# The order of the last five adds and stores of a fused attention and gMLP kernel

## The chip, the core and the metric

The kernel runs on one core of a Trainium2 chip. The metric is the device time of one execution in microseconds, the median of several runs. The core has a matrix engine (TensorE, "PE" in the profile), an elementwise engine (VectorE, "DVE"), an activation engine (ScalarE, "ACT"), GpSimd ("POOL") and a synchronising engine (SyncE, "SP") that here issues nearly all transfers. A name with a q behind it (SPq, DVEq) is the instruction queue of that engine. Each engine works through its own instructions in order, and the engines wait for one another by semaphores.

## What is computed

The input x is 2048 tokens by 512 features in bf16. The reference, cut to what matters:

```python
def reference(A_x, A_wqkv, A_wo, B_x, B_w_in, B_w_sp, B_b_sp, B_w_out):
    x = A_x
    xn = _layernorm(x, axis=-1)
    return x + _A_ref(xn, A_wqkv, A_wo) + _B_ref(xn, B_w_in, B_w_sp, B_b_sp, B_w_out)

# _A_ref: sliding-window attention, 32 heads of 16, window 8, dilation 2
    o = jnp.einsum('bhsw,bhswd->bhsd', attn, vg)
    return (o transposed to (B, S, D)) @ wo

# _B_ref: gMLP
    z = _gelu(x @ w_in); z1, z2 = halves of 688, z2 = _layernorm(z2)
    g = jnp.einsum('ts,bsf->btf', w_sp, z2) + b_sp[None, :, None]
    return (z1 * g) @ w_out
```

So every output tile is a sum of three: the input x, the attention output times `wo`, and the gated product times `w_out`.

## The kernel before

The 2048 tokens are 16 tiles of 128. Four tiles form an output group `o` (0 to 3): tile `tb` of the group is `4 * tb + ORD[o]`. Nothing is scheduled automatically: a long string, `ORDER`, lists the steps, and each step appends its instructions to the queues of the engines that it uses. An engine runs its own instructions in exactly the order in which the steps append them; between engines a semaphore wait is put wherever one reads what another writes.

The steps that make an output group are these.

- `O` (`out_heads`, matmuls at L496) starts four sums of 128 tokens by 512 columns in PSUM and adds the attention part, 16 slices of the head dimension. Tiles 0 and 1 of a group share one PSUM tile `po`, tiles 2 and 3 another. In the last group (`o` = 3) tile 2 and the first `LASTCUT` = 288 columns of tile 3 lie in single-bank tiles called `pa`, and the other 224 columns of tile 3 in `pb`.
- `Or` (`out_rest`, L505) adds the short remainder of the gated product, two pieces.
- `Oh` (`out_half`, with `out_full`, L520) adds the five full pieces of the gated product for two of the four tiles, and with them the sums are complete. `Oh3.0` is for tiles 0 and 1 of the last group, `Oh3.1` for tiles 2 and 3.
- `F` (`out_add`, L510) is an add on VectorE: the sum in PSUM plus the input x (loaded by `xr` into `xr_t`), into `ot_t` in SBUF, as bf16. Tiles of the program called `r_qk` in the profile hold both buffers.
- `s` (`out_store`, L515) issues the transfer of `ot_t` to the output in memory, from SyncE's queue unless another engine is named.

In the last group the second half is different. `out_half(3, 1)` appends, for each of its three pieces in turn, the matmuls, the add and the store at once. One of the stores is issued from ScalarE's queue:

```python
        if o == 3 and h == 1:
            for tb, part, E in ((2, 0, SP), (3, 0, A), (3, 1, SP)):
                out_full(o, tb, part)
                out_add(o, tb, part)
                out_store(o, tb, part, E)
```

The `ORDER` string ends with `Oh3.0 s2.1 Oh3.1 F3.0 F3.1 s3.0 s3.1`. So VectorE's last five adds stand as tile 2, tile 3 (288 columns), tile 3 (224 columns), tile 0, tile 1, and SyncE's last stores stand in the same order, without the 288 columns, which ScalarE's queue issues. TensorE completes the sums in the order tile 0, tile 1, tile 2, tile 3. L687 in the profile is the end of the whole program: the waits for outstanding transfers and the closing drains.

Two more functions are touched: `pair_add` (`a` in the order), which folds four products to two ahead of the logits, and `logits`, which takes the number of products from whether the step's number is in `PAIRED`. All eight are.

Of the kernel before, what the change touches and what calls it, by code (L numbers as in the profile page):

```python
# [11 lines left out]
ALU = mybir.AluOpType  # L12
# [9 lines left out]
C = D // P  # L22
# [5 lines left out]
F = 1376  # L28
# [9 lines left out]


ORD = [1, 2, 3, 0]  # L40
PAIRED = (0, 1, 2, 3, 4, 5, 6, 7)
ORDER = """
z1.2 z2.1 p1.3 z0.3 zg1.2 p0.2 zg2.1 q2.3 zg0.3 p1.1 zs2.1 z1.0 p1.2 qc2.3 q2.1 p1.0 zg1.0 p0.0 z2.2 qc2.1
p0.3 zs1.2 z2.0 p0.1 zg2.2 z0.0 zg2.0 a1 w0 q2.0 zs2.0 zg0.0 a0 z1.1 qc2.0 q2.2 zg1.1 halo zs1.0 p2.3 z3.2
# [12 lines left out]
s0.1 A39 X15 A40 Gi13 X14 A41 G11 A42 Xg14 Xg15 A43 A44 A45 U14 X13 Gi11 A46 O1 Xg13 A47 U11 A48 U10 Or1 A49  # L57
Oh1.0 A50 Oh1.1 F1.0 F1.1 G12 F1.2 U13 s1.2 A51 T10 F1.3 T11 T14 G15 Gi12 T13 U12 A52 s1.3 xr2 A53 A54 s1.0
s1.1 O2 T12 Gi15 A55 A56 A57 Or2 A58 Oh2.0 U15 A59 T15 Oh2.1 F2.0 F2.1 s2.0 O3 F2.2 F2.3 xr3 s2.2 Or3 s2.3
Oh3.0 s2.1 Oh3.1 F3.0 F3.1 s3.0 s3.1  # L60
"""
NZ1 = 8
LASTCUT = 288
# [7 lines left out]
def kernel(  # L71
# [13 lines left out]
    V = nc.vector  # L85
    A = nc.scalar
    G = nc.gpsimd
    PE = nc.tensor
    SP = nc.sync
# [41 lines left out]
    pr = [h.rearrange("p (c w b t) -> p c w b t", w=4, c=C, b=TB) for h in pr_home]  # L131
# [107 lines left out]
    tiles = {}  # L239
# [106 lines left out]
                k_reads[jj].append(prod.ins)  # L346

    def pair_add(g):
        if g not in PAIRED:
            return  # L350
        V.tensor_tensor(pr[g % 3][:, 0:2], pr[g % 3][:, 0:2], pr[g % 3][:, 2:4], ALU.add)  # L351

    def logits(g):
        o, h = g // 2, g % 2
        pl = ps_aux.tile([P, 4, P], F32, name="pl", tag="aux")
        n_c = 2 if g in PAIRED else C
        for c in range(n_c):
            for tb in range(TB):
                PE.matmul(pl[32 * tb:32 * tb + 32, :, :], rsel[:], pr[g % 3][:, c, :, tb, :],  # L359
                          start=(c == 0), stop=(c == n_c - 1), tile_position=(0, 32 * tb))  # L360
        tiles["l", g] = pl
# [146 lines left out]
    def out_add(o, tb, part=0):  # L508
        pc, cs = tiles["o", o][tb][part]
        V.tensor_tensor(ot_t[tb][:, cs], pc, xr_t[tb][:, cs], ALU.add)  # L510

    def out_store(o, tb, part=0, E=SP):
        i = 4 * tb + ORD[o]
        pc, cs = tiles["o", o][tb][part]
        E.dma_start(out2[i * P:(i + 1) * P, cs], ot_t[tb][:, cs])  # L515

    def out_full(o, tb, part=0):
        pc, cs = tiles["o", o][tb][part]
        for m in range(MCH - 2):
            PE.matmul(pc, uT[:, o % 2, m, tb * P:(tb + 1) * P], wout[:, m, cs],  # L520
                      start=False, stop=(m == MCH - 3))

    def out_half(o, h):
        if o == 3 and h == 1:
            for tb, part, E in ((2, 0, SP), (3, 0, A), (3, 1, SP)):
                out_full(o, tb, part)
                out_add(o, tb, part)
                out_store(o, tb, part, E)
        else:
            for tb in (2 * h, 2 * h + 1):  # L530
                out_full(o, tb)


    pwm = ps_mm.tile([P, 2, TBS], F32, name="pwm", tag="mm")
# [110 lines left out]
    def halo_zero():  # L645
# [3 lines left out]
    nw = z2_var(0, 2) + z2_newton(0, 2)  # L649
    st = z2_var(3, 3) + [z2_log, z2_exp]  # L650

    steps = {"z": z2_mm, "zg": z2_gelu, "zs": z2_sq, "q": qk_mm, "qc": qk_cast, "p": prod_c, "a": pair_add,
             "L": logits, "Lc": logits_cast, "V": v_mm, "Vc": v_cast, "X": z1_mm, "Xg": z1_gelu,
             "nw": lambda k: nw[k](), "st": lambda k: st[k](), "N": z2_norm,
             "M": sm_max, "E": sm_exp, "S": lambda h, k: sm_sum(h, k), "R": sm_norm, "mask": add_mask,
             "G": g_mm, "Gi": g_bias, "U": u_mul, "T": u_tr, "A": lambda k: ap[k](),
             "O": out_heads, "Or": out_rest, "Oh": out_half, "F": out_add, "s": out_store,
             "halo": halo_zero, "wo": load_wo, "late": load_late, "xr": load_xr, "w": load_wsp}
    for tok in ORDER.split():
        name = tok.rstrip("0123456789.")  # L660
# [31 lines left out]
```

## Time and profile before

| | |
|---|---|
| median of 5 runs | 206.88 us (206.8 to 207.5) |
| the profiled execution's own time | 206.81 us |
| its span in the profile | 205.1 us |
| TensorE busy | 198.3 us (97%) |
| VectorE busy | 180.7 us (88%) |
| ScalarE busy | 97.4 us (48%) |
| granted TensorE clock, mean | 0.994 |

The span runs from the first to the last recorded instruction of one execution; the time of an execution is somewhat longer, since it contains what lies around the span. A row of the timeline gives start, duration, engine, line of the kernel, operation, and output and input tiles; a bracket behind it says how long the engine was idle before and what ended that. The rows of a queue (SPq, ACTq) give the time in which it issues a transfer, not the transfer's. When the data has landed is told by the list of transfers.

### The profile page before, as it was taken

The numbers are of one execution on the slowest core, as the hardware profiler recorded it, in microseconds if no ns is written. First come the engines' busy times: TensorE is split into PE (matmuls) and PEld (weight loads), VectorE is DVE, ScalarE is ACT, GpSimd is POOL, SyncE is SP. The second block draws the span as 40 slices with busy tenths as digits, with TensorE's granted clock in tenths as the row PEclk, the third lists the DMA queues.
The fourth block names the chain that finished last, engine by engine and source line by source line (L and its number), as shares of the span: only waits on it lengthen the run. The fifth ranks groups of instructions, "written<-read, shape, count | busy, mean of one in ns | idle before, by whom it ended". The sixth has DMA issues, their size and how long they took to land.

```text
span 205.1 us, 4087 instructions
## 1 busy us (share of the span) xinstructions
PE 198.3 (97%) x1699; PEld 125.2 (61%) x1699; DVE 180.7 (88%) x259; ACT 97.4 (48%) x159; POOL 5.8 (3%) x15
## 2 busy tenths in 40 slices
PE   7799999999999999999999999999999999999991
PEld 2589856655566666666566666664566654664650
DVE  4999799899599999879999999999999998599604
ACT  3575989799899786833303845530041230020000
POOL 5000000600000000000000000000000000000000
PEclk9999999999999999999999999999999999999997
DMA  5973447400000894399960599999399000456623
GB/s 150 361 243 76 98 91 252 88 0 0 3 0 3 170 162 83 71 228 211 170 157 8 140 175 213 252 192 191 73 135 243 22 3 0 118 142 171 165 88 104
DMA packets 65826, 25.91 MB, mean 126 GB/s; under 512 B 56208, under 2 KB 65488, under 8 KB 65552
## 3 DMA queue, kind: packets, MB, share of 16 engines
q1 hardware_dynamic: 65360, 25.12, 56.2%
q10 hardware_dynamic: 368, 0.27, 0.5%
q0 software_dynamic: 80, 0.26, 0.5%
q8 instruction: 13, 0.21, 0.5%
q14 instruction: 5, 0.04, 0.1%
HBM read 10.13 MB, written 2.10 MB: 60 GB/s over the span
## 4 chain that ended last, share of the span: by engine, by line
PE 94%; DVE 2%; DMA 1%; ACT 1%; DVEq 0%; issue 0%
PE pg L448 36%; PE pz L235 18%; PE pq L306 13%; PE po L520 8%; PE pv L409 7%; PE po L496 6%; PE pl L359 2%; DMA r_x<-in_A_x_dram 1%; PE pa L520 1%; PE po L505 1%; PE pb L496 1%; PE pt L221 1%; DVE stats L203 1%; ACT xnT L225 1%; DVE r_qk L510 1%; PE pa L306 0%
## 5 line engine op out<-in xcount | busy, mean ns | idle before, releaser
L448 PE MATMUL pg<-z,r_qk 128*128 128x344 bf16 x448 | 67.0, 309 | 0.0
L448 PEld LDWEIGHTS <-r_qk 128*128 128x128 bf16 x448 | 43.8, 98 | 21.8
L235 PE MATMUL pz<-w_z,xnT 128*128 128x344 bf16 x256 | 40.3, 309 | 0.0
L454 ACT ACTIVATE gs<-pg,b_col 128x688 bf16<-128x688 f32 x16 | 13.2, 832 | 53.7 <-PE pg L448 53.6
L423 DVE TENSOR_TENSOR r_pr<-r_x,r_w 128x2048 bf16<-128x2048 bf16 x32 | 38.3, 1220 | 0.4
L427 DVE TENSOR_TENSOR r_pr<-r_pr 128x2048 bf16<-128x2048 bf16 x28 | 33.9, 1218 | 0.1
L235 PEld LDWEIGHTS <-xnT 128*128 128x128 bf16 x256 | 24.8, 98 | 13.9 <-issue 1.2
L340 DVE TENSOR_TENSOR r_pr<-r_qk 128x2048 bf16<-128x2048 bf16 x24 | 28.3, 1221 | 2.5 <-ACT r_qk L316 2.5
L306 PE MATMUL pq<-xnT,r_w 128*128 128x256 bf16 (+1 forms) x176 | 29.0, 316 | 0.3 <-ACT xnT L225 0.3
L306 PEld LDWEIGHTS <-r_w 128*128 128x128 bf16 x184 | 20.1, 114 | 7.4 <-issue 0.4
L316 ACT CAST r_qk<-pq 128x1024 bf16<-128x1024 f32 (+1 forms) x16 | 15.4, 993 | 3.3 <-PE pq L306 3.0
L297 ACT ACTIVATE r_uz<-pz 128x688 bf16<-128x688 f32 x16 | 11.6, 744 | 9.7 <-PE pz L235 9.1
L520 PE MATMUL po<-r_w,r_uz 128*128 128x512 bf16 x70 | 15.8, 380 | 0.0
L409 PE MATMUL pv<-xnT,r_w 128*32 128x512 bf16 x256 | 14.6, 380 | 0.0
L496 PE MATMUL po<-r_lg,r_pr 32*128 32x512 bf16 x224 | 14.5, 375 | 0.0
L520 PEld LDWEIGHTS <-r_uz 128*128 128x128 bf16 x85 | 8.0, 98 | 9.8 <-issue 1.5
L351 DVE TENSOR_TENSOR r_pr<-r_pr 128x4096 bf16<-128x4096 bf16 x6 | 13.6, 2288 | 0.0
L259 ACT ACTIVATE junk<-z 128x688 bf16<-128x688 bf16 x16 | 12.5, 781 | 0.1
L203 DVE BATCH_NORM_STATS2 stats<-r_x 128x6 f32<-128x512 bf16 x16 | 10.8, 673 | 1.7 <-DMA r_x<-in_A_x_dram 1.7
L409 PEld LDWEIGHTS <-r_w 128*32 128x32 bf16 x256 | 9.4, 139 | 4.6 <-issue 0.3
L253 ACT ACTIVATE z<-pz 128x688 bf16<-128x688 f32 x16 | 11.8, 741 | 0.5 <-PE pz L235 0.5
L496 PEld LDWEIGHTS <-r_pr 32*128 32x128 bf16 x272 | 7.6, 93 | 6.5 <-issue 0.9
(80 smaller groups left out, 162.8 us busy)
## 6 DMA issues: line engine op xcount, KB each, us to landing
r_lg<-in_A_wo_dram SPq DMA_DIRECT2D x8, 256.0 KB, 4.4
r_qk<-in_A_x_dram SPq DMA_DIRECT2D x16, 128.0 KB, 2.4
out_dram<-r_qk SPq DMA_DIRECT2D x15, 128.0 KB, 2.1
r_w<-in_A_wqkv_dram SPq DMA_DIRECT2D x3, 512.0 KB, 5.4
r_x<-in_A_x_dram SPq DMA_DIRECT2D x3, 512.0 KB, 6.1
w_z<-in_B_w_in_dram SPq DMA_DIRECT2D x2, 688.0 KB, 6.6
r_w<-in_B_w_out_dram SPq DMA_DIRECT2D x1, 640.0 KB, 5.9
r_x<-in_A_x_dram POOLq DMA_DIRECT2D x1, 256.0 KB, 3.8
```

The lines of the kernel that those rows point to most:

```text
L235: PE.matmul(pz[:, hh, 0:FHALF], xnT[:, kc, i * P:(i + 1) * P], wz[:, kc, hh * FHALF:(hh + 1) * FHALF], start=(kc == 0), stop=(kc == C - 1))
L306: PE.matmul(pq[:, cc, p0 * P:(p0 + b1 - b0) * P], wqk[:, sd, kc, c0 + cc:D:C], xv[:, kc, b0:b1, j, :], start=(kc == 0), stop=(kc == C - 1))
L316: cast = A.copy(dst, pq[:, :, p0 * P:(p0 + b1 - b0) * P].rearrange("p c (b t) -> p c b t", b=b1 - b0))
L340: prod = V.tensor_tensor(pr[g % 3][:, c].rearrange("p w b t -> p b w t"), q3.unsqueeze(2).broadcast_to([P, TB, 4, P]), k4, ALU.mult)
L351: V.tensor_tensor(pr[g % 3][:, 0:2], pr[g % 3][:, 0:2], pr[g % 3][:, 2:4], ALU.add)
L409: PE.matmul(pv[32 * tb:32 * tb + 32, dd, :], wv[:, kc, 2 * d2 + dd, :], xnT[:, kc, tb * TBS:(tb + 1) * TBS], start=(kc == 0), stop=(kc == ...
L423: V.tensor_tensor(pw_t[n], vp[:, :, off:off + P], a_sb[:, slot_w(w), ts].unsqueeze(1).broadcast_to([P, DH, P]), ALU.mult)
L427: V.tensor_tensor(pw_t[n] if dst is None else dst, pw_t[n], pw_t[m], ALU.add)
L448: PE.matmul(pg[:, hh, 0:FHALF], wsp[n][:, k, :], z2[:, k, hh * FHALF:(hh + 1) * FHALF], start=(k == 0), stop=(k == NT - 1))
L454: A.activation(gs[:], tiles.pop(("g", n))[:, :, 0:FHALF], ACT.Identity, bias=b_col[:, i:i + 1])
L496: PE.matmul(pc, op[32 * tb:32 * tb + 32, d, o * P:(o + 1) * P], wo_r[32 * tb:32 * tb + 32, d, cs], start=(d == 8), stop=False, tile_positi ...
L520: PE.matmul(pc, uT[:, o % 2, m, tb * P:(tb + 1) * P], wout[:, m, cs], start=False, stop=(m == MCH - 3))
```

## The change

In `out_half` the special case of the last group goes: it now appends matmuls alone, as for the other groups. The adds and stores of tiles 2 and 3 move to a new step `end`, `last_adds`, which stands at the very end of `ORDER`, behind `F3.0 F3.1 s3.0 s3.1`. On VectorE the last five adds are then tile 0, tile 1, tile 2, tile 3 (288), tile 3 (224). On SyncE the stores of tiles 0 and 1 stand ahead of those of tile 2 and of the 224 columns. ScalarE's queue still issues the store of the 288 columns. `PAIRED` becomes a tuple of the number of products, 2 for each of the eight steps, and a function for a third fold, `pair_add2`, is there but appears in no step of the order.

```diff
-PAIRED = (0, 1, 2, 3, 4, 5, 6, 7)
+CHUNKS = (2, 2, 2, 2, 2, 2, 2, 2)
...
-Oh3.0 s2.1 Oh3.1 F3.0 F3.1 s3.0 s3.1
+Oh3.0 s2.1 Oh3.1 F3.0 F3.1 s3.0 s3.1 end
...
     def pair_add(g):
-        if g not in PAIRED:
-            return
         V.tensor_tensor(pr[g % 3][:, 0:2], pr[g % 3][:, 0:2], pr[g % 3][:, 2:4], ALU.add)
+
+    def pair_add2(g):
+        V.tensor_tensor(pr[g % 3][:, 0], pr[g % 3][:, 0], pr[g % 3][:, 1], ALU.add)
...
-        n_c = 2 if g in PAIRED else C
+        n_c = CHUNKS[g]
...
     def out_half(o, h):
-        if o == 3 and h == 1:
-            for tb, part, E in ((2, 0, SP), (3, 0, A), (3, 1, SP)):
+        for tb in (2 * h, 2 * h + 1):
+            for part in range(len(tiles["o", o][tb])):
                 out_full(o, tb, part)
-                out_add(o, tb, part)
-                out_store(o, tb, part, E)
-        else:
-            for tb in (2 * h, 2 * h + 1):
-                out_full(o, tb)
+
+    def last_adds():
+        for tb, part, E in ((2, 0, SP), (3, 0, A), (3, 1, SP)):
+            out_add(3, tb, part)
+            out_store(3, tb, part, E)
```

The table of steps gains `"b": pair_add2` and `"end": last_adds`.

More of the change, by code (lines that the diff above doesn't have):

```diff
@@ L650 @@
     st = z2_var(3, 3) + [z2_log, z2_exp]
-    steps = {"z": z2_mm, "zg": z2_gelu, "zs": z2_sq, "q": qk_mm, "qc": qk_cast, "p": prod_c, "a": pair_add,
+    steps = {"z": z2_mm, "zg": z2_gelu, "zs": z2_sq, "q": qk_mm, "qc": qk_cast, "p": prod_c, "a": pair_add, "b": pair_add2,
              "L": logits, "Lc": logits_cast, "V": v_mm, "Vc": v_cast, "X": z1_mm, "Xg": z1_gelu,
@@ L656 @@
              "G": g_mm, "Gi": g_bias, "U": u_mul, "T": u_tr, "A": lambda k: ap[k](),
-             "O": out_heads, "Or": out_rest, "Oh": out_half, "F": out_add, "s": out_store,
+             "O": out_heads, "Or": out_rest, "Oh": out_half, "F": out_add, "s": out_store, "end": last_adds,
              "halo": halo_zero, "wo": load_wo, "late": load_late, "xr": load_xr, "w": load_wsp}
```

## The prediction

> **What bounds the kernel now.** I read four views: the page for the whole, the timeline of the last ten microseconds engine by engine, the landing times of the last stores, and SyncE's waits after its last issue.
>
> The page first, for what the span hangs on:
>
> ```profile
> span 205.1 us, 4087 instructions
> ...
> PE 198.3 (97%) x1699; PEld 125.2 (61%) x1699; DVE 180.7 (88%) x259; ACT 97.4 (48%) x159; POOL 5.8 (3%) x15
> ...
> PE 94%; DVE 2%; DMA 1%; ACT 1%; DVEq 0%; issue 0%
> ```
>
> TensorE carries 94% of the chain of waits, so up to the last matmul only TensorE's work counts. The change touches none of it. What it can move lies behind the last matmuls, so the timeline of that stretch decides. The columns are start, duration, engine, line, operation and tiles; a row merges a run of like instructions (the ten `pa` matmuls are five of 512 columns and five of 288).
>
> ```profile
> 192.07 1.29 DVE L510 TENSOR_TENSOR r_qk<-po,r_qk 128x512 bf16<-128x512 f32 x2 [0.56 <-PE po L520]
> 199.46 1.07 DVE L510 TENSOR_TENSOR r_qk<-pa,r_qk 128x512 bf16<-128x512 f32 x2 [6.10 <-PE pa L520]
> 200.55 0.39 DVE L510 TENSOR_TENSOR r_qk<-pb,r_qk 128x224 bf16<-128x224 f32 x1
> 200.86 1.28 DVE L510 TENSOR_TENSOR r_qk<-po,r_qk 128x512 bf16<-128x512 f32 x2
> ...
> 196.01 2.33 PE L520 MATMUL po<-r_w,r_uz 128*128 128x512 bf16 x10
> 198.18 1.85 PE L520 MATMUL pa<-r_w,r_uz 128*128 128x512 bf16 x10
> 199.87 0.64 PE L520 MATMUL pb<-r_w,r_uz 128*128 128x224 bf16 x5
> ```
>
> TensorE finishes `po` (token tiles 0 and 1) at 196.01 + 2.33 = 198.34, `pa` (tile 2 and the first 288 columns of tile 3) at 200.03 and `pb` (the last 224 columns) at 200.51. VectorE adds in another order: it is idle for 6.10 us until `pa`'s first half is done at 199.46, adds `pa`, `pa`, `pb`, and only at 200.86 starts the two `po` adds, 2.5 us after their sums were complete. It ends at 202.14, 1.63 us after TensorE. From 198.34 to 199.46 it has nothing to do. The first row belongs to group 2 and shows how soon an add follows its matmuls: it starts at 192.07, as that tile ends, with TensorE already in the next group.
>
> The stores come next. For each of SyncE's four, the issue row and then the landing row of its own short window (count, KB, us from issue to landing, left out where the trace has no landing):
>
> ```profile
> 200.18 0.33 SPq L515 DMA_DIRECT2D out_dram<-r_qk  x1
> ...
> 200.97 0.33 SPq L515 DMA_DIRECT2D out_dram<-r_qk  x1
> ...
> out_dram<-r_qk SPq DMA_DIRECT2D x1, 56.0 KB, 1.5
> ...
> 201.57 0.33 SPq L515 DMA_DIRECT2D out_dram<-r_qk  x1
> ...
> out_dram<-r_qk SPq DMA_DIRECT2D x1, 128.0 KB, 2.1
> ...
> 202.17 0.33 SPq L515 DMA_DIRECT2D out_dram<-r_qk  x1
> ...
> out_dram<-r_qk SPq DMA_DIRECT2D x1, 128.0 KB, 1.8
> ...
> SPq L687 <- DMA out_dram<-r_qk: 1.4, 2, 1.1
> ```
>
> Each store is issued 0.03 us after its add ends (200.55 + 0.39 = 200.94, then 200.97; 202.14, then 202.17). The last, tile 1, lands at 202.17 + 1.8 = 204.0. SyncE's closing wait (L687) is for these stores, and the span ends 205.1 - 204.0 = 1.1 us after the landing, in closing semaphores and drains. So the end is: last add, 0.03, landing time of the last store, 1.1.
>
> **The change part by part.** In the order of the built program TensorE keeps all 3,400 rows in their places; only line numbers differ. `pair_add`'s test and `CHUNKS` give the same instructions as before, and the new step `b` is never in the order: these cost nothing because nothing of them is executed. What moves:
>
> VectorE's last five adds become po, po, pa 512, pa 288, pb. The durations come from the rows above. Two 512 adds take 1.28 us and one alone 0.68, so the second starts 0.60 after the first. The 224 add starts at 200.55 and the next at 200.86, so its step is 0.31. By the slope between them (0.29 for 288 columns) the 288 add's step is an estimated 0.37.
> - First po add: both tiles lie in one PSUM tile, and the wait stands on the first add alone, as in group 2. So it waits for the end of both, 198.34, and starts at 198.38 (I allow the 0.04 us seen from 200.51 to 200.55).
> - Second po add 198.98. `pa` 512 at 199.58: `pa` allowed it at 199.46, so it is 0.12 late. `pa` 288 at 200.18, where its matmuls were done at 200.03: 0.15 late.
> - `pb` at 200.18 + 0.37 = 200.55. TensorE frees it at 200.55 too. The two adds put ahead have been absorbed by the idle 1.1 us and by the gaps in which VectorE waited for TensorE. Without that cover they would cost 2 x 0.60 us, and the change would gain only the last store's shorter landing.
>
> The last add ends at 200.94 instead of 202.14: 1.20 us earlier.
>
> The stores: SyncE issues tile 0 at 199.09, tile 1 at 199.69, tile 2 at 200.30; ACT issues the 288 columns at about 200.67, some 0.1 later than before (200.56); SyncE issues the 224 columns at 200.97, as now. Both moved stores pass three others: tile 2 and the 224 columns on SyncE's queue and the 288 columns on ACT's. An issue takes 0.33 us and the issues are 0.6 apart, so SyncE is free each time. The data of a 128 KB store occupied the DMA engines for about 0.45 us (299 GB/s in the window 201.05 to 201.50), which fits between issues. In before the 224-column store already went out behind the 128 KB and 72 KB stores, and landed 1.5 us after its issue; I take that row, since its two neighbours are the same ones. SyncE's last landing is then 200.97 + 1.5 = 202.5 instead of 204.0.
>
> The new waits: the second po add also waits for the old store out of its buffer, issued at 196.13; even with the 3.4 us that the slowest late store took it is there by 199.53, 0.55 after the add wants to start. TensorE has nothing left that waits for VectorE.
>
> Sum: 1.20 from the last add and 0.3 from the landing (1.8 against 1.5), 1.5 us in all; the closing 1.1 stays. That is 205.1 - 1.5 = 203.6 us of span. The profiled execution took 206.81 us, 1.7 around its span, so it would take 205.3; the median of the five runs, 206.88, lies 0.07 above it. I round up to 205.4.
>
> **Two rules against the rows.** The rows say 1.5 us for the 56 KB store and 1.8 for the 128 KB one. The Trainium skill, "DMA: Bandwidth & Descriptors", section "Anatomy of one DMA — SWDGE (gpsimd) path", fits a DMA as about 2.0 us fixed plus bytes over 436 GB/s, measured on another issue path. That makes an estimated 2.13 and 2.30, hence 0.17 instead of 0.3 for the landing, and 1.37 instead of 1.5 in all. Two of the three landings shown lie under the fit's fixed 2.0 alone, so I use the rows; the rule is one reason for rounding up. Against the change speaks the same page's "Specifications": writes below 512 B are read, modified and written. The store that is now last has rows of 448 B. The page names no price. If it doubled the landing to 3.0, the last landing would be 204.0, and the change would be worth nothing. But the 1.5 us was measured on these very rows, so any such price is already in it.
>
> **Rivals.**
> - *The tail of the DMA engines eats part of it.* One instruction-fetch packet runs beside the last stores in before (a DMA queue of kind "instruction" moves one packet between 202.0 and 204.3), and the two 128 KB stores landed 2.1 and 1.8 us after issue, though of one size. If that fetch moves forward with the tail and falls on the short store, or if it queues behind four close stores, its landing becomes 1.8: 1.2 gained, 205.7. For: the 0.3 spread. Against: the 1.5 us was measured behind the same two stores.
> - *The first po add waits one group too long*, for the end of `pa`'s first half at 199.42, because TensorE's signal is counted coarsely. Then adds start at 199.46, 200.06, 200.66, 201.26, 201.63; `pb` ends at 202.02, its store lands at 203.55, and only 0.45 is gained: 206.4. Against: the row at 192.07.
> - *Slower: the same signal comes with TensorE's last matmul.* Then all five adds start after 200.55: the last starts at 200.55 + 0.60 + 0.60 + 0.60 + 0.37 = 202.72, ends 203.11, is issued 203.14, lands 204.64, 0.6 later than now: 207.5. It decides from the point where the first add starts over 1.5 us late, after 199.9. For: the adds are queued in order, so one late release holds all five. Against: in group 2 the `po` add was released while TensorE ran on.
> - *Nothing changes*: the end would have to hang on something other than the stores. The closing wait of 1.1 us on them speaks against it. 206.9.
>
> **How the numbers follow.** The forecast, 205.4, has 0.78; the DMA tail, 205.7, 0.12; the wait of one group, 206.4, 0.04; no change, 0.03; slower, 0.03. This kernel's measurement can tell about 0.2%, or 0.4 us, from no change. The first two cases and most of the third are faster by more than that: 0.93; same 0.04; slower 0.03. The five runs before reach 0.6 us above their median, so the range goes from 205.0 (landing shorter still, 0.3 below the sum) to 206.1 (the DMA tail with a median 0.4 high), leaving out the last three cases.
>
> **What would show it.** Right: VectorE's idle row before the first po add ends at about 198.4; two po adds, then `pa`, `pa`, `pb` without idle; the `pb` add still at 200.55 to 200.6; SyncE's last issue at 200.97, of 56 KB, with a landing near 1.5; span 203.6. Wrong: the first po add released after 199; the `pb` add starting well after 200.6; a landing of the 56 KB store of 2 us or more; or an issue row on SyncE much longer than 0.33.

## The result and the profile after

The changed kernel takes 205.31 us (median), the kernel before 206.97 us in the same measurements. The ratio is 0.9926, with a 95% interval from 0.9913 to 0.9939: 0.74% faster, or about 1.5 us of 206.97. (The ratio is that of the fast runs alone, not the quotient of the two medians, and leaves out one run of before that took 740.8 us.) The profiled executions have spans of 203.7 and 205.1 us, 1.4 apart. The forecast was 205.4 with a range from 205.0 to 206.1.

The page of the changed kernel, for the whole:

```profile
span 203.7 us, 4088 instructions
...
PE 198.5 (97%) x1699; PEld 125.3 (62%) x1699; DVE 180.7 (89%) x259; ACT 97.4 (48%) x159; POOL 5.8 (3%) x15
...
PE 94%; DVE 2%; DMA 2%; ACT 1%; issue 0%; ACTq 0%; DVEq 0%
```

Busy times are as before to 0.2 us, so nothing was saved in work. In the timeline of the tail (start, duration, engine, line, operation, tiles; the source has grown by a line, so L510 is now L511, L515 is L516, L520 is L521 and L687 is L688) the order is another:

```profile
198.45 1.29 DVE L511 TENSOR_TENSOR r_qk<-po,r_qk 128x512 bf16<-128x512 f32 x2 [5.02 <-PE po L521]
199.66 1.04 DVE L511 TENSOR_TENSOR r_qk<-pa,r_qk 128x512 bf16<-128x512 f32 x2
200.62 0.39 DVE L511 TENSOR_TENSOR r_qk<-pb,r_qk 128x224 bf16<-128x224 f32 x1
...
196.08 2.33 PE L521 MATMUL po<-r_w,r_uz 128*128 128x512 bf16 x10
198.25 1.86 PE L521 MATMUL pa<-r_w,r_uz 128*128 128x512 bf16 x10
199.94 0.64 PE L521 MATMUL pb<-r_w,r_uz 128*128 128x224 bf16 x5
```

VectorE's idle time is 1.1 us shorter, because `po` and not `pa` ends it (5.02 instead of 6.10). The two `po` adds fill the time up to 199.66, and `pb`'s add starts at 200.62, 0.04 after TensorE ends at 199.94 + 0.64 = 200.58. TensorE itself is 0.07 later than in before. The last add ends at 201.01, where in before it ended at 202.14: 1.13 us.

Two of SyncE's stores, in the same two views as in the prediction (issue row, then KB and us to landing), and SyncE's closing wait:

```profile
200.37 0.33 SPq L516 DMA_DIRECT2D out_dram<-r_qk  x1
...
out_dram<-r_qk SPq DMA_DIRECT2D x1, 128.0 KB, 1.7
...
201.04 0.33 SPq L516 DMA_DIRECT2D out_dram<-r_qk  x1
...
out_dram<-r_qk SPq DMA_DIRECT2D x1, 56.0 KB, 1.5
...
SPq L688 <- DMA out_dram<-r_qk: 1.0, 2, 0.7
```

The last store is the one of 56 KB. It goes out at 201.04 instead of 202.17 and lands 1.54 us later instead of 1.85 (the second decimal from the trace's records). From there to the end of the span it is 1.08, against 1.07 in before. So the span's 1.4 us are 1.13 from the last add and 0.3 from the landing.

### The profile page after: what moved, and what is told of

Its sections match the earlier page's. It is cut to its first block, busy times and chain, and to the rows that moved or that the text cites. A ratio compares the mean times of both kernels' runs of the same rounds, so it can differ in the third digit from the quotient of the medians.

```text
span 203.7 us, 4088 instructions
## 1 busy us (share of the span) xinstructions
PE 198.5 (97%) x1699; PEld 125.3 (62%) x1699; DVE 180.7 (89%) x259; ACT 97.4 (48%) x159; POOL 5.8 (3%) x15
## 4 chain that ended last, share of the span: by engine, by line
PE 94%; DVE 2%; DMA 2%; ACT 1%; issue 0%; ACTq 0%; DVEq 0%
PE pg L449 37%; PE pz L235 18%; PE pq L306 13%; PE po L521 8%; PE pv L410 7%; PE po L497 6%; PE pl L360 2%; DMA r_x<-in_A_x_dram 2%; DVE r_qk L511 1%; PE po L506 1%; PE pb L497 1%; PE pt L221 1%; ACT xnT L225 1%; PE pa L306 0%; DVE stats L203 0%
## 5 line engine op out<-in xcount | busy, mean ns | idle before, releaser
L521 PE MATMUL po<-r_w,r_uz 128*128 128x512 bf16 x70 | 15.8, 380 | 0.0
L511 DVE TENSOR_TENSOR r_qk<-po,r_qk 128x512 bf16<-128x512 f32 x14 | 9.1, 687 | 6.3 <-PE po L521 6.3
L521 PEld LDWEIGHTS <-r_uz 128*128 128x128 bf16 x85 | 8.0, 98 | 9.8 <-issue 1.5
```

## Experiments

Theory A: the last add ends 1.2 us earlier, because two adds moved into time in which VectorE was idle, and the last store is now a short one. Rival B: the order in which the stores go out is what counts. Each variant below is an edit of the changed kernel unless it says otherwise. Ratios are against before, measured in the same series.

**The adds alone (e1).** Tiles 2 and 3 have their steps ahead of the stores of tiles 0 and 1:

```diff
-Oh3.0 s2.1 Oh3.1 F3.0 F3.1 s3.0 s3.1 end
+Oh3.0 s2.1 Oh3.1 F3.0 F3.1 end s3.0 s3.1
```

> The adds stand in the changed order, SyncE's stores in the order of before (tile 2, the 224 columns, tile 0, tile 1). Theory A (the gain is the last add ending 1.2 us earlier plus a last store that is short): the last add ends at 201.0, but tile 0 and tile 1 are then issued one after the other behind the 224-column store, at about 201.4 and 201.8, and the last lands 1.8 later, at 203.6. Span 204.7, gain 0.4 us on before. Rival B (the gain comes from the order in which the stores go out, not from the adds): no gain, 205.1.

Measured: ratio 1.0006 [0.9988, 1.0024], span 205.5. That is no gain, and 0.8 us more than theory A said. The adds did what they should (`pb`'s ended 0.43 us after TensorE's last matmul, as in the changed kernel). SyncE's last two rows, and their landing:

```profile
201.58 0.92 SPq L516 DMA_DIRECT2D out_dram<-r_qk  x2
...
out_dram<-r_qk SPq DMA_DIRECT2D x2, 128.0 KB, 2.4
```

The last store goes out at 202.07, 0.27 later than I had put it: TensorE is 0.15 later in this execution than in the changed kernel, and the issue just ahead of it takes 0.45 instead of 0.33. Its landing, 2.33 instead of 1.8, makes up the rest. In the trace's records fifteen of the sixteen parts of this store, each of which signals its own landing, had arrived by 203.87, and the sixteenth came at 204.41, 0.54 later; I come back to that below. The time agrees with rival B's number, so this run alone does not decide against it.

**The stores alone (e2).** The adds of tiles 2 and 3 first, as in before; then the stores in the changed order:

```diff
-Oh3.0 s2.1 Oh3.1 F3.0 F3.1 s3.0 s3.1 end
+Oh3.0 s2.1 Oh3.1 end
...
-        for tb, part, E in ((2, 0, SP), (3, 0, A), (3, 1, SP)):
+        for tb, part in ((2, 0), (3, 0), (3, 1), (0, 0), (1, 0)):
             out_add(3, tb, part)
+        for tb, part, E in ((0, 0, SP), (1, 0, SP), (2, 0, SP), (3, 0, A), (3, 1, SP)):
             out_store(3, tb, part, E)
```

> The stores stand in the changed order, the adds in the order of before. Theory A: the first store waits for tile 0's add, which still ends at 201.5, and holds the others behind it: issues at 201.57, 202.17, 202.55 and 202.95; the last, short one lands 1.5 later at 204.5. Span 205.5, 0.4 us slower than before. Rival B (order of the stores): most of the gain of 1.4 us is there, span below 204.2.

Measured: ratio 1.0038 [1.0024, 1.0052], span 205.8. Slower, as theory A says, and by 0.3 us of span more than it said: the last two issues stand back to back and take longer, so that the last store goes out at 203.08 instead of 202.95, and it lands after 1.64 instead of 1.5. Rival B is out. Tile 0's store stands first in SyncE's queue and is issued at 201.62, because its add is the fourth of five. Tile 2 and the 224 columns, whose data has long been ready, stand behind it and tile 1 (the last row is the issues of these two):

```profile
200.91 1.28 DVE L511 TENSOR_TENSOR r_qk<-po,r_qk 128x512 bf16<-128x512 f32 x2
...
201.62 0.33 SPq L516 DMA_DIRECT2D out_dram<-r_qk  x1
...
202.60 0.91 SPq L516 DMA_DIRECT2D out_dram<-r_qk  x2
```

Both halves of the change together gain 1.5 us, the one half nothing and the other half less than nothing. For the stores alone the reason is the waiting queue. In the nothing of the adds alone about 0.5 us is the late sixteenth part, so not all of it is due to the order.

**One tile ahead (e3).** `F3.0 s3.0 end F3.1 s3.1` in place of the last steps.

> Half of the change: tile 0's add and store stand first, tile 1's last. Theory A: tile 0's add falls into VectorE's idle time, pa and pb keep their places, tile 1's add starts right behind pb at 200.93, ends 201.61, its store is issued at 201.64 and lands 1.8 later at 203.4. Span 204.5, gain 0.6 us: one add's step, and nothing of the landing term, since the last store is a 128 KB one. Rival C (the gain is all or nothing, from which store is last): below 0.2 us.

Measured: span 204.5, as theory A put it, with tile 1's add at 200.92 and its store landing 1.8 after 201.63. The timed runs scattered: median 206.50 against 206.85, ratio 0.9992 [0.9969, 1.0014], so the time does not show a gain. The profile shows 0.6 us, about one add's step, for one moved add; so rival C is out by the profile alone.

**A third add in the cover (e4).** `F3.1` stands twice, so tile 1's add is done twice.

> The changed kernel with tile 1's add done twice, so that VectorE has three 512-column adds ahead of pa. Theory A says the cover (VectorE's 1.1 us of idle time plus its waits for TensorE) is used up by two adds: the third costs its whole step, pb's add starts at 201.3, span 204.4, 0.6 to 0.7 us more than the changed kernel. Rival D (there is cover left, TensorE's last matmul sets the end): no more than 0.1 us over the changed kernel, 203.7.

Measured: ratio 0.9959 [0.9944, 0.9973], span 204.4, which is 0.8 us over the changed kernel.

```profile
198.49 2.01 DVE L511 TENSOR_TENSOR r_qk<-po,r_qk 128x512 bf16<-128x512 f32 x3 [5.02 <-PE po L521]
200.43 1.04 DVE L511 TENSOR_TENSOR r_qk<-pa,r_qk 128x512 bf16<-128x512 f32 x2
201.38 0.38 DVE L511 TENSOR_TENSOR r_qk<-pb,r_qk 128x224 bf16<-128x224 f32 x1
```

`pb`'s add starts 0.76 after the changed kernel's. The third add costs its whole step and 0.1 more (three take 2.01, two took 1.29): it writes the same tile as the second and starts only after that has ended, while the first two overlap by 0.08. The cover had no room for a third add; rival D is out.

**Tile 0's add earlier still (e7).** The add of tile 0 directly behind tile 0's matmuls:

```diff
                 out_full(o, tb, part)
+                if o == 3 and tb == 0:
+                    out_add(o, tb)
...
-Oh3.0 s2.1 Oh3.1 F3.0 F3.1 s3.0 s3.1 end
+Oh3.0 s2.1 F3.1 s3.0 s3.1 Oh3.1 end
```

> The changed kernel with tile 0's add put directly behind tile 0's own matmuls, ahead of tile 1's, which lie in the same PSUM tile. The built program then has TensorE's first matmul of tile 1 wait for that add. Theory A: VectorE starts a microsecond earlier, which the tail cannot use because pb's add waits for TensorE anyway; TensorE stands for the add (0.7) and the signals, so everything behind comes 0.7 to 0.8 us later, span 204.4. Rival F (VectorE's chain of five adds is the bound and a head start helps): span at or below 203.6.

Measured: ratio 0.998 [0.997, 0.9989], span 204.5, 0.9 us over the changed kernel.

```profile
197.33 0.69 DVE L511 TENSOR_TENSOR r_qk<-po,r_qk 128x512 bf16<-128x512 f32 x1 [3.94 <-PE po L521]
...
198.07 1.24 PE L521 MATMUL po<-r_w,r_uz 128*128 128x512 bf16 x5 [0.78 <-DVE r_qk L511]
199.15 1.85 PE L521 MATMUL pa<-r_w,r_uz 128*128 128x512 bf16 x10
200.84 0.64 PE L521 MATMUL pb<-r_w,r_uz 128*128 128x224 bf16 x5
```

VectorE starts 1.1 us sooner, and TensorE pays: tile 1's matmuls write the PSUM tile that the add reads, and TensorE stands idle 0.78 us for it (bracket). It ends at 200.84 + 0.64 = 201.48, 0.90 later than in the changed kernel, and everything behind it is later by as much. Rival F is out: in the changed kernel VectorE needs no head start, and TensorE must not wait.

**Where tile 3 is cut (e5, e6).** `LASTCUT` 128 and 384 instead of 288.

> The changed kernel with tile 3 cut at column 128 instead of 288: the last add has 384 columns (about 0.56 us by the slope of the measured adds) and the last store has 96 KB and rows of 768 B. Theory A (a store's landing grows with its size, no extra price for the 448 B rows): the add ends at 201.2 instead of 201.0, the landing is about 1.7 instead of 1.55, span 204.0, 0.3 us over the changed kernel. Rival E (rows below 512 B pay a price): the landing is no longer than 1.55, perhaps shorter, and the span grows by 0.2 at most or not at all.

> The changed kernel with tile 3 cut at column 384: the last add has 128 columns, the last store 32 KB and rows of 256 B. Theory A: VectorE now bounds the tail, pa's second add starts at 200.3, pb's at 200.8, ends at 201.05, as in the changed kernel; the landing is about 1.45 to 1.5: span 203.6, within 0.1 of the changed kernel. Rival E (short rows pay): the landing is 1.8 or more, span 203.9 or more.

Measured: at 128, ratio 0.9993 [0.9971, 1.0015], span 204.8; at 384, ratio 0.995 [0.993, 0.9969], span 203.7. The second fits theory A in the span, though the 32 KB store landed after 1.67, not 1.45 to 1.5. The 96 KB store of tile 3's other columns had been issued only 0.19 us before it, so it probably waited for that one's data; this was not separated. A price for short rows does not show: a store of the same shape, rows of 256 B and 32 KB, took 1.56 in the variant e11 below. The first is 0.8 over what theory A allowed, again through a landing:

```profile
201.25 0.33 SPq L516 DMA_DIRECT2D out_dram<-r_qk  x1
...
out_dram<-r_qk SPq DMA_DIRECT2D x1, 96.0 KB, 2.4
```

**The landing that is too long (e9, e10, e11).** Every trace so far has one odd packet near the end: 8 KB on the queue of kind "instruction", which takes one of the 16 DMA engines for 0.32 to 0.74 us. In e1, e5 and before it runs ahead of or beside the data of the last stores. The DMA queues of e5 from 201.9 to 204.6 (packets, MB, share of 16 engines):

```profile
q1 hardware_dynamic: 144, 0.10, 11.4%
q14 instruction: 1, 0.01, 1.7%
```

Here fifteen of the sixteen parts of the last store had landed by 202.87, and the sixteenth came at 203.70. From run to run the packet follows ScalarE: its start lies 1.2 to 1.5 us after the end of ScalarE's store issue in all of the ten executions whose 288 columns (or their counterpart) go out from ScalarE. Theory G says that this packet holds a part of the store in flight. A transfer on ScalarE's queue is not enough by itself: in the changed kernel ScalarE issues one 0.3 us ahead of the last store, which still lands in 1.54. Theory G can be tried by giving ScalarE nothing to issue:

```diff
-        for tb, part, E in ((2, 0, SP), (3, 0, A), (3, 1, SP)):
+        for tb, part, E in ((2, 0, SP), (3, 0, SP), (3, 1, SP)):
```

This was done to before (e9), to the changed kernel (e10) and to the cut at 128 (e11).

> The kernel before with all its stores on SyncE, the 288 columns too. Open is why the two 128 KB stores of before landed 2.1 and 1.8 us after issue, where 128 KB stores elsewhere take 1.7. Theory G: an 8 KB packet of instruction fetch, which starts 1.2 to 1.5 us after ScalarE has issued its store (ScalarE reaching its program's end), holds one DMA engine and with it one sixteenth of the store in flight. With nothing for ScalarE to issue, the fetch comes long before the tail, both stores land in about 1.7, and the span is 204.9, 0.15 us under before. Rival H (the fetch has its own time, or stores of the tail wait on one another): landings as in before, span 205.1.

> The changed kernel with all its stores on SyncE. Theory G: its fetch starts at 202.35, just after the last store's data, so it costs nothing there and taking it away brings nothing; SyncE has one more issue between, which may hold the last store by 0.1. Span 203.7 to 203.8. Against before with SyncE alone: 1.2 us, so that the part of the gain that is not due to the fetch is the earlier add and the smaller last store. Rival H: 203.7 as well; this run is the counterpart of the one before, not a test by itself.

> The cut at column 128 with all stores on SyncE. With ScalarE's store its last landing took 2.4 us against 1.7 expected. Theory G: the fetch started at 202.17, in the midst of the last store's data; with the fetch gone the landing is 1.65 to 1.7 and the span 204.0, 0.7 us less than with ScalarE's store. Rival E' (a 96 KB last store or its 768 B rows are slow by themselves): landing 2.4, span 204.8.

The clearest is e11, ratio 0.9954 [0.9941, 0.9966], span 203.9 against e5's 204.8. Its last store, and the DMA queues in the stretch from 202.0 to its end at 203.9, in which the instruction queue no longer appears:

```profile
201.15 0.40 SPq L516 DMA_DIRECT2D out_dram<-r_qk  x1
...
out_dram<-r_qk SPq DMA_DIRECT2D x1, 96.0 KB, 1.7
...
q1 hardware_dynamic: 144, 0.10, 16.2%
```

The same store lands in 1.7 instead of 2.4, so neither its size nor its rows were slow. With the one late part of sixteen, this leaves the packet. In one thing theory G was wrong: the packet did not come long before the tail but behind it, at 204.6, after the last landing (and so in e9, e10 and e12). In all fourteen executions it starts 1.0 to 1.3 us after a closing instruction of ScalarE: the drain behind its store where it has one, otherwise its first closing semaphore wait. This fits a packet that follows ScalarE's own progress; what calls for it is not shown.

In e9 the landings of before's two last stores fall from 2.1 and 1.8 to

```profile
out_dram<-r_qk SPq DMA_DIRECT2D x1, 128.0 KB, 1.8
...
out_dram<-r_qk SPq DMA_DIRECT2D x1, 128.0 KB, 1.7
```

The span is 205.0 and the ratio 0.9992 [0.9958, 1.0025], too wide to show the 0.1 us by time. In e10 (ratio 0.9951 [0.9939, 0.9963]) the span is 204.2, 0.4 over what I expected: TensorE ends 0.32 later in that execution, and the last store is issued 0.25 us after its add ends instead of 0.03, because SyncE now has the 288 columns to issue just before. ScalarE's queue saves these 0.22 us in the trace. Against e9, where SyncE issues all too, the span is 0.8 shorter, or 1.1 without TensorE's 0.35; the medians are 206.63 and 205.66. So most of the gain is there without the packet.

**The last store on the last semaphore (e8, e12).** SyncE's closing waits stand in a fixed order of eight transfer semaphores. Three more issues at an early point move the last store to the last of them; e12 has SyncE alone as well.

```diff
-        SP.dma_start(wout[:, 0:MCH - 2, :], B_w_out[0:FULL, :].rearrange("(m p) n -> p m n", p=P))
+        for m0, m1 in ((0, 2), (2, 3), (3, 4), (4, 5)):
+            SP.dma_start(wout[:, m0:m1, :], B_w_out[m0 * P:m1 * P, :].rearrange("(m p) n -> p m n", p=P))
```

> The changed kernel with one early load (the five full pieces of w_out) issued in four pieces instead of one, so that the semaphores of the last stores move on by three places of eight. SyncE's closing waits stand in the order of those semaphores; the last store's is now the last of them instead of three before it. If the three waits behind it (about 0.06 us each) are real work that stands behind the landing, the span falls by about 0.2 us to 203.5; if they are not, it stays at 203.7. Three more issues at an early point (0.33 to 0.43 us each on SyncE) may cost something on the way; I expect nothing of it at the end.

> Candidate for the shortest: the changed kernel with the last store on the semaphore that is waited for last (0.19 us less tail in the trace) and all stores on SyncE, so that no fetch can fall on them. Expected span 203.5 to 203.6 and a median of 205.1 to 205.3. Theory G adds that runs in which the last store is held by the fetch disappear, so the spread above the lowest time should shrink; rival H: no difference to the changed kernel.

Measured: e8 205.20 us, ratio 0.9932 [0.9912, 0.9952], span 203.6; e12 205.31 us, ratio 0.9942 [0.9922, 0.9962], span 203.5. From the last landing to the end it is 0.89 us in both, against 1.08 in the changed kernel, so the three waits are real. Their 0.19 us are 0.09% of the time, and the intervals of both overlap that of the changed kernel. Neither is shown to beat it. Nor did e12's times lie closer together (205.19 to 206.96), so the scatter has other causes than the packet.

## Why the prediction was right

- *What bounds the end.* The chain "last add, 0.03, landing, closing 1.1" holds in the changed kernel with 0.03, 1.54 and 1.08. e4 and e7 move the last add, by 0.75 and 0.89 us, and leave the stores' order alone: the span grows by 0.76 and 0.88.
- *The first `po` add waits for both tiles, until 198.38.* It started at 198.45, with TensorE 0.07 later. The rivals that had the signal come late are out by that row. e7 shows the other side of the shared PSUM tile: an add put between the two tiles makes TensorE wait.
- *The cover.* The steps were forecast as 0.60, 0.60, 0.60 and 0.37, and measured as 0.61, 0.60, 0.60 and 0.37; `pb`'s add was to start at 200.55, as TensorE frees it, and started at 200.62 with TensorE at 200.58. e4 shows that the cover ended there.
- *The old store of the second `po` add.* Here the working has a slip. Its worst case, the old store out of the buffer by 199.53, is 0.55 after that add's start, so it would have held that add and the three behind it; the sum put this at nothing. In the changed kernel's records that store was issued at 195.78 and had landed by 197.62, so nothing waited. The term was nothing because the store was quick, not because its worst case was covered.
- *The last add 1.20 earlier.* Measured 1.13: the rest is TensorE's 0.07.
- *The stores ahead do not hold the last one.* Issues of 0.33 us, 0.6 apart, as forecast, and a landing of 1.54 against the 1.5 taken from before's row. The price for rows of 448 B does not show, and the fit's fixed 2.0 us is too long for all five stores of this tail (1.5 to 1.7 in the trace's records).
- *The landing's 0.3.* The size was right, the reason only half. The prediction took 1.8 against 1.5 as what a 128 KB and a 56 KB store need. Without the instruction packet a 128 KB store takes 1.71 (e9), so 0.17 is size, the difference that the fit gave and the prediction set aside. The other 0.14 was the packet, which in before held the last two stores: the sixteenth part of the last one came 0.16 after the fifteenth. In the changed kernel's profiled execution it starts at 202.35, when the last store's data is through (202.22). The rival of the DMA tail had named the packet and the danger, and the prediction had no row that told where the packet would fall. That it missed the store by 0.13 us was luck; in e1 and e5 it did not, and its sixteenth part cost 0.54 and 0.83 us.

## What to carry to other kernels

At the end of a kernel, let the adds stand in the order in which their sums become complete, and the stores in the order in which the adds end, with a small one last (here worth 0.17 us). Count what the idle time ahead can hold: two adds were free here and the third cost its whole step. Turning only the stores round lost time here, since a queue waits for its first entry; turning only the adds round gained nothing that could be measured.

## What was not expected of the hardware

An 8 KB instruction packet starts 1.2 to 1.5 us after ScalarE's last store issue and takes one of the 16 DMA engines for up to 0.74 us. A store has landed only with its sixteenth part, so the last landing was 2.4 us in e5, where it met the packet, and 1.7 in e11, where it did not. With no store on ScalarE the packet came after the last landing. The closing waits behind the last store's semaphore cost about 0.06 us each.
